# Pooled attention and a max-out feed-forward layer on one core: where key turns and one token turn stand in a hand-written order, and which engine copies the keys

## The chip, the cores and the metric

The kernel runs on one core of one Trainium2 chip. The metric is the device time of one execution in microseconds (us). The kernel before took 227.16 us, the median of three runs (226.39 to 227.36). All times inside an execution are counted from the start of the profiled span.

## The reference

The inputs are q, k and v of shape (8 batches, 8 heads, 576 tokens, 64), and four weights. Keys and values are averaged over groups of 8 tokens, which leaves 72 pooled keys and values per head; then comes ordinary attention, and a layer that takes the largest of three products.

```python
k_p = k.reshape(B, H, Sp, pool, D).mean(axis=3)
v_p = v.reshape(B, H, Sp, pool, D).mean(axis=3)
attn = softmax(q @ k_p.transpose(0, 1, 3, 2) / sqrt(D))
x = (attn @ v_p).transpose(0, 2, 1, 3).reshape(B * S, H * D)     # 4608 x 512
h = maximum(maximum(x @ w1, x @ w2), x @ w3)                     # 4608 x 768
out = h @ w_out                                                  # 4608 x 512
```

## The kernel before

**Two streams of work.** Attention goes by batch b (0 to 7, 576 tokens each). The feed-forward layer goes by blocks n of 512 tokens (0 to 8). The attention of a batch feeds the block or two behind it. The program is written out in issue order: every engine takes its instructions in the order of the program, and waits inside them are semaphores.

**The steps of a batch b.** GpSimd loads `q`, `k`, `v` with a cast to 2 bytes (L73 to L100) and sums keys and values over each group of 8 in the helper at L157 (tiles `half`, then `kp` and `vp`). The step `T` (L349) turns the queries on the way by a transposing DMA on SyncE's queue, `qT<-qb`. The step `k` (L207) is the key turn: three TensorE transposes of `kp` into a PSUM tile `pkt` (L202), then four copies of `pkt` into `kz` (L213), each 64 partitions by 288 elements. `s0`, `s3`, `s6` are the scores (`psc`, L226) with their exponentials on ScalarE (`et`, L231). `v0` to `v4` are five chunks of 128 tokens: eight matmuls into `pav` (L302), a reciprocal (L310) and a product (L312) on VectorE, which gives `xn`. `x0` to `x4` turn each chunk into the token ring `xT`: for batches up to 2 with four TensorE transposes into `pxt` (L293) and a ScalarE copy (L296), for later batches with a transposing DMA on SyncE's queue (L287).

**The steps of a block n.** `h` is one product of the hidden layer: four matmuls of 512 columns into a tile `pw` (L419); of each pair the first is taken out of PSUM by ScalarE (`t`, L425), the second by VectorE (`hT`, L427). A block from 2 on has twelve. The output stage is the digits 1, 2, 6, 7, 5, 3, 4: seven products of ten matmuls each (L765). Products 1, 6, 5 and 3 use the PSUM bank `oA` one after another and are copied out by ScalarE (L776); product 2 uses `oB`, and 7 and 4 use `oC`, which VectorE adds to the output (L779). `a` and `b` steps are VectorE differences that feed the products, `f` steps are sums of weights. A minus behind a name issues the TensorE part, a plus the copy out of PSUM; with neither sign, both come at once.

**The order.** `MIDDLE` (L949) holds a string for each of the blocks 1 to 5, and `middle(n)` (L982) reads it out. A name without a batch means batch n+1. `q7<`, `k7<`, `v7<` issue loads on GpSimd, which wait for the last hidden product issued so far and for the last turned queries. `!` says that the next sum on GpSimd waits for VectorE's last difference. After block 5 another string, `ORDER`, takes over.

**PSUM** has 8 banks. In this part of the program `att` is two tiles of two banks (scores, `pav`, `pxt` of batch 2, and `pkt`), `pw` three tiles of one bank (hidden products, `oB` and `oC`), `tr` one bank (`oA`). The tiles of a tag go round in order: a new one waits until the one two (`att`) or three (`pw`) places earlier has been read.

Of the kernel before, what the change touches and what calls it, by code (L numbers as in the profile page):

```python
# [14 lines left out]
def kernel(  # L15
# [11 lines left out]
    nc = tc.nc  # L27
# [3 lines left out]
    B, H, S, D = q.shape  # L31
# [167 lines left out]
    def keys(b, tag):  # L199
        pkt = psum([128, 3, 96], BF16, name="pkt", tag=tag[0], bufs=tag[1])  # L200
        for i in range(3):
            nc.tensor.transpose(pkt[:, i, :],  # L202
                                kps[b][:, 2 * i:2 * i + 2, :].rearrange("p i d -> p (i d)"),
                                ident[0:96, 0:96])
        return pkt

    def turn_k(b):  # L207
        pkt = keys(b, ATT if len(pools) < 3 else SC)

        def put():  # L210
            for par, evac in enumerate((nc.vector.tensor_copy, nc.scalar.copy)):
                for odd in range(2):
                    (evac if b > 2 else nc.vector.tensor_copy)(  # L213
                        out=kz_all[b % 2][par][64 * par:64 * par + 64, :, 0:Sp].rearrange(
                             "p h (r i t) -> p h r i t", i=3, t=2)[:, :, :, :, odd],
                        in_=pkt[64 * odd:64 * odd + 64].rearrange(
                             "p i (h r) -> p h r i", r=12))

        return put
# [100 lines left out]
    ATT = ("att", 2)  # L320
    ATT0, ONE = ("att", 3), ("one", 2)
    SC = ("sc", 2)
# [6 lines left out]
    def parts(name, begin):  # L329

        if name[-1] == "+":
            parked[name[:-1]].pop(0)()
        elif name[-1] == "-":
            parked.setdefault(name[:-1], []).append(begin())
        else:
            begin()()

    def do(b, steps):

        for name in steps.split():
            i = int(name[1:].rstrip("+-") or 0)
            if name[0] in "qQ":
                turn_q(b, *QS[i], nc.vector.tensor_copy if name[0] == "Q"
                       else nc.scalar.copy, TR)
            elif name[0] == "T":
                qTs[b] = sb2.tile([128, 2 * NG, 128], BF16, name="qT", tag="qT")
                turned[:] = [nc.sync.dma_start_transpose(  # L349
                    out=qTs[b], in_=qbs[b].rearrange("p hp t d -> p (hp t d)"))]  # L350
            elif name[0] == "k":
                parts(f"{b}:{name}", lambda: turn_k(b))
            elif name[0] == "K":
                fold_k(b, nc.vector)
            elif name[0] == "s":
                if i == 0 and name[-1] != "+":
                    new_et(b)
                if len(pools) == 3:
                    parts(f"{b}:{name}", lambda: scores_flat(b, i))
                elif name[-1] == "+":  # L360
                    parked[b, i].pop(0)()
                else:
                    ends = scores(b, {0: (0, 1, 2), 3: (4, 5, 3), 6: (6, 7)}[i])
                    if name[-1] == "-":
                        parked[b, i] = ends
                    else:
                        for end in ends:
                            end()
            elif name[0] == "d":
                for j in range(2):  # L370
                    sub_w(i, j, j + 1)
            elif name[0] == "S":
                next(out_sums, None)
            elif name[0] == "z":
                for par in range(2):
                    nc.vector.memset(kz_all[1][par], 0.0)
            elif name[0] == "w":
                turn_w(i, nc.scalar.copy if i % 2 else nc.vector.tensor_copy)
            elif name[0] == "v":
                parts(f"{b}:{name}", lambda: values(b, CHUNKS[i][0]))  # L380
            else:
                turn_x(b, *CHUNKS[i], xns[b, CHUNKS[i][0]], TR if b == 1 else ATT,
                       nc.vector.tensor_copy if name[0] == "X" else nc.scalar.copy)

    w1T = const.tile([128, JCH, C], F16, name="w1T", tag="w1T")
# [490 lines left out]

    folding = {}

    def pool_step(n, name):

        what, b = name[0], int(name[1])
        if name[2:] == "<":
            load = {"k": lambda: load_k(b, nc.gpsimd), "v": lambda: load_v(b, nc.gpsimd),
                    "q": lambda: load_q(b)}[what]
            op = load()
            for x in (mms[-1], *turned):
                after([op], x)
            return
        if (what, b) not in folding:
            if what == "k":  # L890
                new_kp(b)
                folding[what, b] = fold_steps(nc.gpsimd, kts[b], kps[b], parts=2)
            else:
                folding[what, b] = fold_steps(nc.gpsimd, vts[b], vp_all[:, b, :, 0:D],
                                                  parts=2)
        for _ in range(int(name[3:])):
            op = next(folding[what, b])
            for x in held:
                after([op], x)
            held.clear()  # L900
# [14 lines left out]
    def weave():  # L915

        products, seen, outs = {}, {}, out_seven(5)
        for name in ORDER.split():
            if name == "F":
                next(tiles)  # L920
            elif name == "vpool":
                held[:] = gate
                pool_step(5, "v7+4")
            elif name[0] == "b":
                sums_of(5, name)
            elif name == "H":
# [19 lines left out]
                else:  # L946
                    parts(name, begin)

    MIDDLE = {  # L949
        1: """  # L950
            h- q4< k4< h+ 1:x2 1:v4- h- h- v4< h+ 1:v4+ h+ h- 1:x3 h- h+ h+ h- 1:x4 h+ h- k-
            h- h+ h+ q0 h h- k+ h+ h q1 h s0- s0+ s0+ q2 h- s0+ h- s0+ h+ b1 S q3 h+ h- S S
            3:T S h+ a3 s3- a1 s3+ s3+ h- s3+ h- h+ h+ a2 h- s3+ a4 s6- s6+ 1- s6+ h+ b3 b2
            b4 v0 2- 1+ 6- x0 v1 7- v2- 6+ x1 5- 2+ 7+ v2+ ! k3+4 v3- v3+2 v3+ 5+ v4 3- x2
            4- x3 3+ 4+ x4
        """,
        2: """
            h k5< k- h- k+ h+ a1 a3 h- a2 f a4 f ! v3+2 v5< h+ f s0- s0+ s0+ s0+ h- h- h- h+
            h+ s0+ h- h+ s3- h+ h- f s3+ h- s3+ h+ h- s3+ b1 s3+ s6- h+ s6+ h- h+ h- s6+ !
            k4+2 h+ h+ b2 b3 b4 ! k4+2 1- 4:T v0- 1+ v1- v0+ x0 2- v1+ 6- v2- 7- x1 2+ 7+  # L960
            v4+2 6+ v2+ 5- v3- 5+ v3+ x2 x3 v4 x4 3- 4 3+
        """,
        3: """
            k- q5< k+ a3 k6< h a1 h- h- h+ a2 s0- f a4 ! v4+2 s0+ s0+ f h- h+ s0+ h+ s0+ h-
            h- h+ h+ s3- h- v6< h+ h s3+ s3+ s3+ s3+ h- b1 h- h+ h+ s6- s6+ ! k5+2 h h- s6+
            1- h+ b2 b3 b4 1+ ! k5+2 v5+2 v0- 2- v0+ x0 v1 6- 2+ x1 6+ 7- 5:T 7+ v2- 5- v2+
            x2 v3- 5+ v3+ v4 x3 3 x4 4
        """,
        4: """
            h- q6< h+ k- h- k+ a1 a2 f h+ h- a3 a4 ! v5+2 h- f h+ k7< h+ s0- s0+ h- h- s0+  # L970
            s0+ h+ s0+ h+ 6:T h- s3- h+ s3+ s3+ s3+ h- s3+ h+ h- b1 h+ h ! k6+2 s6- s6+ h h
            b3 b2 b4 s6+ ! k6+2 1- v6+2 v0 2- 1+ x0 v1- 6- v1+ 2+ x1 v2 7- 6+ 5- x2 v3 6:k-
            x3 7+ 5+ 3- 6:k+ v4 x4 4- 3+ 4+
        """,
        5: """
            h q7< a1 v7< h- a2 h- a3 h+ h+ a4 ! v6+2 h- s0- s0+ h+ s0+ h- s0+ s0+ h- h- k7+4
            h+ h+ s3- h+ 7:T s3+ h- s3+ h- s3+ s3+ h+ s6- h+ s6+ s6+ h h- v0 h+ h- x0 v1- h+
            v1+ x1
        """}
    folds = iter([f for wi in range(1, 3) for f in [fold_w(wi)] * 4])  # L980

    def middle(n):  # L982

        pieces, outs, out_tiles = hidden(n), None, project(n)
        for name in MIDDLE[n].split():
            if name[0] == "h":
                parts(name, lambda: next(pieces))
            elif name == "F":
                next(out_tiles)
            elif name == "f":  # L990
                next(next(folds))
            elif name == "!":
                held[:] = gate
            elif name[0].isdigit() and name[1:] in ("", "+", "-"):
                outs = outs or out_seven(n)
                parts(f"o{name}", lambda: outs(int(name[0]), 0, 1))
            elif name[0] in "ab":
                sums_of(n, name)
            elif name[2:3] == "<" or name[2:3] == "+" and name[3:]:
                pool_step(n, name)  # L1000
            else:
                b, _, step = name.rpartition(":")
                do(int(b or n + 1), step)
        assert next(pieces, None) is None

    tt_all.append(const.tile([128, 4, 5, HALF], F16, name="tt", tag="tt"))
    for n in range(1, 6):
        middle(n)
    assert next(folds, None) is None
    pad2 = const.tile([128, 3, 2, HALF], F16, name="pad2", tag="k16")  # L1010
    pad3 = ld.tile([128, 8, 2, HALF], F16, name="pad3", tag="vt")
# [47 lines left out]
```

## Time and profile before

| what | value |
|---|---|
| median of three runs | 227.16 us |
| the profiled execution's own time | 227.08 us |
| its span on the core | 225.4 us |
| TensorE matmul busy | 212.3 us (94%) |
| VectorE busy | 161.4 us (72%) |
| ScalarE busy | 120.3 us (53%) |
| GpSimd busy | 140.9 us (63%) |
| granted TensorE clock | 1.0 |
| key copies (L213) | 18 on VectorE of 478 ns, 10 on ScalarE of 476 ns |
| query turns by DMA (L349) | 5, from 4.0 to 10.2 us from issue to landing |

Three views are read below. The chain of waits follows the work that ended last back to the start, and tells at each step what released it. The timeline lists merged instructions: start, length, engine, line, operation, tiles, count, and in square brackets how long the engine was idle before and on whom it waited. The page's list of DMA issues gives the time from issue to landing. Matmul rows overlap, since each row includes the time until its result has landed: a group's start and the next group's start tell more than the length of the row.

### The profile page before, as it was taken

What the parts mean: (1) busy time and instruction counts of PE and PEld (TensorE: products, weight loads), DVE (VectorE), ACT (ScalarE), POOL (GpSimd) and SP (SyncE); (2) the same over time, 40 slices, a digit from 0 to 9 for tenths busy, and PEclk for the clock granted to TensorE, in tenths of its full rate; (3) what the DMA queues carried; (4) which work ended last, traced back from release to release, by engine and by line L of the source; (5) the groups of instructions that cost most, each with busy time, mean ns of one, the idle gap of its engine ahead of it and who ended that gap; (6) DMA issues with size and microseconds to landing.
All of it is one profiled execution on the core that took longest, in us unless ns stands there. A gap on an engine that the chain in (4) does not pass through costs nothing.

```text
span 225.4 us, 4876 instructions
## 1 busy us (share of the span) xinstructions
PE 212.3 (94%) x1884; PEld 147.1 (65%) x1885; DVE 161.4 (72%) x314; ACT 120.3 (53%) x233; POOL 140.9 (63%) x121
## 2 busy tenths in 40 slices
PE   6688999999999999999999999999799999999993
PEld 2477744458658645964685468547589667788882
DVE  3668898036997796776679668729767977878940
ACT  2267524855883576237724842693694445564330
POOL 7974300999939969775885769794292903881020
PEclk9999999999999999999999999999999999999999
DMA  6999999999649999649967999699530755200265
GB/s 179 209 197 197 211 203 209 202 168 230 115 105 156 168 176 247 122 61 214 252 85 154 221 202 151 86 236 166 109 56 19 163 102 113 47 0 3 66 198 159
DMA packets 47303, 33.55 MB, mean 149 GB/s; under 512 B 26992, under 2 KB 42288, under 8 KB 47280
## 3 DMA queue, kind: packets, MB, share of 16 engines
q0 software_dynamic: 16944, 16.98, 47.8%
q1 hardware_dynamic: 29888, 15.87, 31.1%
q10 hardware_dynamic: 448, 0.39, 0.7%
q8 instruction: 15, 0.25, 0.5%
q14 instruction: 8, 0.07, 0.1%
HBM read 34.60 MB, written 9.44 MB: 195 GB/s over the span
## 4 chain that ended last, share of the span: by engine, by line
PE 58%; DMA 17%; DVE 10%; POOL 7%; ACT 3%; issue 3%; ACTq 0%; POOLq 0%; DVEq 0%
PE pw L419 17%; PE oA L765 12%; DMA vt<-in_v_dram 8%; PE oC L765 6%; PE pA L842 5%; DMA mw<-in_moe_w_dram 4%; DMA qT<-qb 4%; PE oB L765 3%; PE pC L842 3%; PE pav L302 2%; PE po L471 2%; PE psc L226 2%; POOL half L163 2%; DVE kz L213 2%; DVE tt L664 1%
## 5 line engine op out<-in xcount | busy, mean ns | idle before, releaser
L419 PE MATMUL pw<-xT,mw 128*128 128x512 f16 (+1 forms) x336 | 68.5, 349 | 0.3 <-ACT xT L296 0.2
L419 PEld LDWEIGHTS <-mw 128*128 128x128 f16 x336 | 30.7, 98 | 26.1 <-issue 1.8
L163 POOL TENSOR_TENSOR half<-vt 72x1024 f32<-72x1024 f16 (+1 forms) x12 | 29.1, 2444 | 20.8 <-DMA vt<-in_v_dram 13.3
L427 DVE TENSOR_TENSOR hT<-t,pw 128x512 f16<-128x512 f16 (+1 forms) x42 | 25.3, 608 | 19.1 <-PE pw L419 11.3
L231 ACT ACTIVATE et<-psc 72x512 f16<-72x512 f32 (+2 forms) x66 | 33.9, 571 | 6.7 <-PE psc L226 6.5
L165 POOL TENSOR_TENSOR half<-half 72x1024 f32<-72x1024 f32 (+1 forms) x13 | 28.1, 2165 | 12.6 <-DVE tt L664 5.2
L425 ACT ACTIVATE t<-pw 128x512 f16<-128x512 f32 (+1 forms) x42 | 22.6, 538 | 15.1 <-PE pw L419 14.5
L312 DVE TENSOR_TENSOR xn<-pav,rcp 128x512 f16<-128x512 f32 x40 | 27.6, 691 | 1.4
L776 ACT COPY osb<-oA 128x512 f32<-128x512 f32 x20 | 11.7, 587 | 20.1 <-PE oA L765 19.9
L851 ACT CAST pad<-pA 128x512 f16<-128x512 f32 x27 | 15.1, 585 | 11.7 <-PE pA L842 9.1
L765 PEld LDWEIGHTS <-tt 128*128 128x128 f16 x200 | 18.8, 98 | 2.1
L163 POOL TENSOR_TENSOR half<-ktFalse 96x768 f32<-96x768 f16 (+1 forms) x11 | 19.3, 1773 | 0.6 <-issue 0.5
L226 PEld LDWEIGHTS <-kz 64*128 64x128 bf16 (+1 forms) x161 | 8.9, 95 | 12.4 <-issue 7.2
L302 PEld LDWEIGHTS <-et 72*128 72x128 f16 x320 | 14.9, 98 | 3.0 <-issue 1.1
L302 PE MATMUL pav<-vp,et 72*128 72x65 f16 x320 | 16.3, 194 | 0.6 <-POOL vp L167 0.3
L310 DVE RECIPROCAL rcp<-pav 128x8 f32<-128x8 f32 x40 | 8.1, 201 | 11.3 <-PE pav L302 11.2
L842 PEld LDWEIGHTS <-sw 128*128 128x128 f16 x144 | 13.8, 98 | 2.7 <-issue 0.2
L822 DVE SCALAR_TENSOR_TENSOR hT<-pad 128x512 f16<-128x512 f16 x18 | 14.0, 785 | 1.1 <-ACT pad L855 0.5
L819 DVE TENSOR_TENSOR pad<-pad,pC 128x512 f16<-128x512 f16 x18 | 12.3, 681 | 3.5 <-PE pC L842 2.7
L226 PE MATMUL psc<-qT,kz 64*128 64x256 bf16 (+5 forms) x138 | 13.3, 263 | 1.0 <-DVE qT L197 0.9
L616 POOL TENSOR_TENSOR pad<-xT 128x256 f16<-128x256 f16 x8 | 5.5, 687 | 13.1 <-DMA xT<-xn 13.1
L765 PEld LDWEIGHTS <-hT 128*128 128x128 f16 x126 | 12.3, 98 | 1.4
(122 smaller groups left out, 400.6 us busy)
## 6 DMA issues: line engine op xcount, KB each, us to landing
out_dram<-osb SPq DMA_DIRECT2D x32, 128.0 KB, 4.6
ktFalse<-in_k_dram POOLq DMA_DIRECT2D x7, 576.0 KB, 9.1
qb<-in_q_dram POOLq DMA_DIRECT2D x7, 576.0 KB, 7.6
vt<-in_v_dram POOLq DMA_DIRECT2D x7, 576.0 KB, 11.8
out_dram<-osb SPq DMA_DIRECT2D x11, 256.0 KB, 6.8
mw<-in_moe_w_dram POOLq DMA_DIRECT2D x9, 256.0 KB, 9.2
ktTrue<-in_k_dram SPq DMA_DIRECT2D x3, 384.0 KB, 5.1
out_dram<-ob SPq DMA_DIRECT2D x8, 128.0 KB, 2.9
```

Of the source, the lines that this page charges most:

```text
L163: yield e.tensor_tensor(out=f[:, at], in0=t[:, at, 0:4, :], in1=t[:, at, 4:8, :], op=ALU.add)
L165: yield e.tensor_tensor(out=f[:, :, 0:2, :], in0=f[:, :, 0:2, :], in1=f[:, :, 2:4, :], op=ALU.add)
L226: nc.tensor.matmul(out, kz_all[b % 2][f % 2][rows, h, :], qTs[b][rows, n + i0:n + i1, 64 * (h % 2):64 * (h % 2) + 64], start=True, stop=True)
L231: nc.scalar.activation(out=out, in_=in_, func=FT.Exp, scale=1.0 / 64.0)
L302: nc.tensor.matmul(pav[:, h // 4, 65 * (h % 4):65 * (h % 4) + 65], ets[b][:, h, c0:c0 + 128], vp_all[:, b, h, :], start=True, stop=True)
L312: nc.vector.tensor_tensor(out=xn, in0=pv[:, :, :, 0:D], in1=rcp.to_broadcast([128, 2, 4, D]), op=ALU.mult)
L419: mm = nc.tensor.matmul(pw, w_sb[wi][:, kc, bass.ts(jc, 128)], x[:, kc], start=(kc == 0), stop=(kc == KCH - 1))
L425: yield lambda t=t, pw=pw: nc.scalar.activation(out=t, in_=pw, func=FT.Relu)
L427: yield lambda t=t, pw=pw: nc.vector.tensor_tensor(out=hT[:, jc, c0:c1], in0=t, in1=pw, op=ALU.max)
L765: nc.tensor.matmul(p, left, right, stop=(r == 4), skip_group_check=True, start=(i in FIRST and r == 0 and (m == 0 or n == LAST)))
L842: mm = nc.tensor.matmul(p[:, w], a[:, kc, bass.ts(g, 128)], b[:, kc, :], start=(i in FIRST and w + kc == 0), stop=(w + kc == 2), skip_grou ...
L851: nc.scalar.copy(out=kept(i, g), in_=p)
```

## The change

Four things change; the loads, the sums, the products and all arithmetic stay as they are.

1. The key turns of batches 4, 5 and 6 take their PSUM tile from `pw` in place of `att`, and all four of their copies are on ScalarE, where two were on VectorE and two on ScalarE. Batches 3 and 7 keep two and two, earlier ones four on VectorE.
2. These three key turns stand elsewhere, and are no longer in two parts. Batch 4's moves from behind block 2's output stage to behind `v4` of batch 3, ahead of block 2's product 3. Batch 5's moves from behind the first hidden product of block 4 to behind `v4` of batch 4, ahead of block 3's product 3. Batch 6's moves by a little: it stays ahead of block 4's product 3, and `v4` of batch 5 now stands ahead of that product too.
3. The token turn `x2` of batch 2 moves from behind block 1's product 3 to ahead of it (and ahead of `v4`), and takes its PSUM tile from `pw`.
4. In batch 2, `v1` and `x0` change places.

The five strings become one with the block's number ahead of a slash; the steps are otherwise the same and in the same order. The core of the diff, with the strings cut to the stretches that differ (the old ones written with the same block and batch numbers):

```diff
+    KP = (4, 5, 6,)
+
     def turn_k(b):
-        pkt = keys(b, ATT if len(pools) < 3 else SC)
+        pkt = keys(b, PW if b in KP else SC if len(pools) == 3 else ATT)
...
-            for par, evac in enumerate((nc.vector.tensor_copy, nc.scalar.copy)):
+            for par in range(2):
                 for odd in range(2):
-                    (evac if b > 2 else nc.vector.tensor_copy)(
+                    (nc.vector.tensor_copy if b < 3 else nc.scalar.copy if par or b in KP
+                     else nc.vector.tensor_copy)(
...
-                turn_x(b, *CHUNKS[i], xns[b, CHUNKS[i][0]], TR if b == 1 else ATT,
+                turn_x(b, *CHUNKS[i], xns[b, CHUNKS[i][0]],
+                       TR if b == 1 else PW if (b, i) == (2, 2) else ATT,
...
-  1/6- 2:x0 2:v1 1/7- 2:v2-
+  1/6- 2:v1 2:x0 1/7- 2:v2-
...
-  1/5+ 2:v4 1/3- 2:x2 1/4- 2:x3 1/3+ 1/4+ 2:x4 2/h
+  1/5+ 2:x2 2:v4 1/3- 1/4- 2:x3 1/3+ 1/4+ 2:x4 2/h
...
-  2/5+ 3:v3+ 3:x2 3:x3 3:v4 3:x4 2/3- 2/4 2/3+ 4:k- q5< 4:k+ 3/a3 k6< 3/h
+  2/5+ 3:v3+ 3:x2 3:x3 3:v4 4:k 3:x4 2/3- 2/4 2/3+ q5< 3/a3 k6< 3/h
...
-  3/5+ 4:v3+ 4:v4 4:x3 3/3 4:x4 3/4 4/h- q6< 4/h+ 5:k- 4/h- 5:k+
+  3/5+ 4:v3+ 4:v4 5:k 4:x3 3/3 4:x4 3/4 4/h- q6< 4/h+ 4/h-
...
-  5:x2 5:v3 6:k- 5:x3 4/7+ 4/5+ 4/3- 6:k+ 5:v4 5:x4 4/4- 4/3+ 4/4+ 5/h
+  5:x2 5:v3 4/7+ 4/5+ 6:k 5:x3 5:v4 4/3- 5:x4 4/4- 4/3+ 4/4+ 5/h
```

More of the change, by code (lines that the diff above doesn't have):

```diff
@@ L877, with pool_step @@
     folding = {}
-    def pool_step(n, name):
+    def pool_step(name):
         what, b = name[0], int(name[1])
@@ L922, in weave @@
                 held[:] = gate
-                pool_step(5, "v7+4")
+                pool_step("v7+4")
             elif name[0] == "b":
@@ L947, in weave @@
                     parts(name, begin)
[L949 to L979, printed above, removed]
@@ L980 @@
-    folds = iter([f for wi in range(1, 3) for f in [fold_w(wi)] * 4])
[L982 to L990, printed above, removed]
+    MIDDLE = """
+        1/h- q4< k4< 1/h+ 1:x2 1:v4- 1/h- 1/h- v4< 1/h+ 1:v4+ 1/h+ 1/h- 1:x3 1/h- 1/h+ 1/h+
+        1/h- 1:x4 1/h+ 1/h- 2:k- 1/h- 1/h+ 1/h+ 2:q0 1/h 1/h- 2:k+ 1/h+ 1/h 2:q1 1/h 2:s0-
+        2:s0+ 2:s0+ 2:q2 1/h- 2:s0+ 1/h- 2:s0+ 1/h+ 1/b1 S 2:q3 1/h+ 1/h- S S 3:T S 1/h+ 1/a3
+        2:s3- 1/a1 2:s3+ 2:s3+ 1/h- 2:s3+ 1/h- 1/h+ 1/h+ 1/a2 1/h- 2:s3+ 1/a4 2:s6- 2:s6+ 1/1-
+        2:s6+ 1/h+ 1/b3 1/b2 1/b4 2:v0 1/2- 1/1+ 1/6- 2:v1 2:x0 1/7- 2:v2- 1/6+ 2:x1 1/5- 1/2+
+        1/7+ 2:v2+ ! k3+4 2:v3- v3+2 2:v3+ 1/5+ 2:x2 2:v4 1/3- 1/4- 2:x3 1/3+ 1/4+ 2:x4 2/h
+        k5< 3:k- 2/h- 3:k+ 2/h+ 2/a1 2/a3 2/h- 2/a2 f 2/a4 f ! v3+2 v5< 2/h+ f 3:s0- 3:s0+
+        3:s0+ 3:s0+ 2/h- 2/h- 2/h- 2/h+ 2/h+ 3:s0+ 2/h- 2/h+ 3:s3- 2/h+ 2/h- f 3:s3+ 2/h-
+        3:s3+ 2/h+ 2/h- 3:s3+ 2/b1 3:s3+ 3:s6- 2/h+ 3:s6+ 2/h- 2/h+ 2/h- 3:s6+ ! k4+2 2/h+
+        2/h+ 2/b2 2/b3 2/b4 ! k4+2 2/1- 4:T 3:v0- 2/1+ 3:v1- 3:v0+ 3:x0 2/2- 3:v1+ 2/6- 3:v2-
+        2/7- 3:x1 2/2+ 2/7+ v4+2 2/6+ 3:v2+ 2/5- 3:v3- 2/5+ 3:v3+ 3:x2 3:x3 3:v4 4:k 3:x4 2/3- 2/4 2/3+ q5< 3/a3 k6< 3/h 3/a1 3/h- 3/h- 3/h+ 3/a2 4:s0- f 3/a4 ! v4+2 4:s0+
+        4:s0+ f 3/h- 3/h+ 4:s0+ 3/h+ 4:s0+ 3/h- 3/h- 3/h+ 3/h+ 4:s3- 3/h- v6< 3/h+ 3/h 4:s3+
+        4:s3+ 4:s3+ 4:s3+ 3/h- 3/b1 3/h- 3/h+ 3/h+ 4:s6- 4:s6+ ! k5+2 3/h 3/h- 4:s6+ 3/1- 3/h+
+        3/b2 3/b3 3/b4 3/1+ ! k5+2 v5+2 4:v0- 3/2- 4:v0+ 4:x0 4:v1 3/6- 3/2+ 4:x1 3/6+ 3/7-
+        5:T 3/7+ 4:v2- 3/5- 4:v2+ 4:x2 4:v3- 3/5+ 4:v3+ 4:v4 5:k 4:x3 3/3 4:x4 3/4 4/h- q6< 4/h+ 4/h- 4/a1 4/a2 f 4/h+ 4/h- 4/a3 4/a4 ! v5+2 4/h- f 4/h+ k7< 4/h+ 5:s0- 5:s0+
+        4/h- 4/h- 5:s0+ 5:s0+ 4/h+ 5:s0+ 4/h+ 6:T 4/h- 5:s3- 4/h+ 5:s3+ 5:s3+ 5:s3+ 4/h- 5:s3+
+        4/h+ 4/h- 4/b1 4/h+ 4/h ! k6+2 5:s6- 5:s6+ 4/h 4/h 4/b3 4/b2 4/b4 5:s6+ ! k6+2 4/1-
+        v6+2 5:v0 4/2- 4/1+ 5:x0 5:v1- 4/6- 5:v1+ 4/2+ 5:x1 5:v2 4/7- 4/6+ 4/5- 5:x2 5:v3 4/7+ 4/5+ 6:k 5:x3 5:v4 4/3- 5:x4 4/4- 4/3+ 4/4+ 5/h q7< 5/a1 v7< 5/h- 5/a2 5/h- 5/a3
+        5/h+ 5/h+ 5/a4 ! v6+2 5/h- 6:s0- 6:s0+ 5/h+ 6:s0+ 5/h- 6:s0+ 6:s0+ 5/h- 5/h- k7+4 5/h+
+        5/h+ 6:s3- 5/h+ 7:T 6:s3+ 5/h- 6:s3+ 5/h- 6:s3+ 6:s3+ 5/h+ 6:s6- 5/h+ 6:s6+ 6:s6+ 5/h
+        5/h- 6:v0 5/h+ 5/h- 6:x0 6:v1- 5/h+ 6:v1+ 6:x1
@@ L991, in middle @@
+    """
+    folds = iter([f for wi in range(1, 3) for f in [fold_w(wi)] * 4])
+    def middle():
+        pieces, outs = {}, {}
+        for name in MIDDLE.split():
+            n, _, step = name.rpartition("/")
+            n = int(n or 0)
+            if step[0] == "h":
+                if n not in pieces:
+                    pieces[n] = hidden(n)
+                parts(name, lambda: next(pieces[n]))
+            elif step == "f":
                 next(next(folds))
-            elif name == "!":
+            elif step == "S":
+                next(out_sums)
+            elif step == "!":
@@ L993, in middle @@
                 held[:] = gate
[L994 to L1000, printed above, removed]
-            else:
-                b, _, step = name.rpartition(":")
-                do(int(b or n + 1), step)
@@ L1004, in middle @@
-        assert next(pieces, None) is None
+            elif n and step[0].isdigit():
+                if n not in outs:
+                    outs[n] = out_seven(n)
+                parts(name, lambda: outs[n](int(step[0]), 0, 1))
+            elif step[0] in "ab":
+                sums_of(n, step)
+            elif step[2:3] == "<" or step[2:3] == "+" and step[3:]:
+                pool_step(step)
+            else:
+                b, _, step = step.rpartition(":")
+                do(int(b), step)
@@ L1006 @@
+        assert all(next(p, None) is None for p in pieces.values())
     tt_all.append(const.tile([128, 4, 5, HALF], F16, name="tt", tag="tt"))
-    for n in range(1, 6):
-        middle(n)
+    middle()
     assert next(folds, None) is None
```

## The prediction

> **What bounds the kernel now.** I read the page first: TensorE is busy for 94% of the span at a granted clock of 1.0. So I asked next for what TensorE waited on, from 56 us (the end of block 0) to 160 us, which covers all that the change touches. Columns: total us, times, longest.
>
> ```profile
> PE psf L226 <- DMA qT<-qb: 1.6, 1, 1.6
> PE oA L765 <- ACT osb L776: 0.7, 4, 0.3
> ```
>
> There are two kinds: one long wait for turned queries, and four equal short ones in the output stage. The chain of waits (start, length, what) says which of them sets the end:
>
> ```profile
> 148.84 1.67 PE pw L419 x8
> 150.51 9.21 DMA qT<-qb
> 159.85 0.38 PE psf L226 x2
> ```
>
> The chain is almost only TensorE from 80 to 150 us, then leaves it for 9.21 us. TensorE goes on working meanwhile, arrives about 1.6 us too early and stands. So time saved on TensorE before 158 us counts only as far as this transfer comes earlier too. The timeline shows what starts it:
>
> ```profile
> 138.28 0.42 PE L302 MATMUL pav<-vp,et 72*128 72x65 f16 x8
> 138.54 0.29 PE L202 MATMUL pkt<-ident,kp 96*128 96x96 bf16 x3
> 139.11 0.60 PE L765 MATMUL oA<-so,xT 128*128 128x256 f16 x4 [0.28 <-ACT osb L776]
> 141.56 3.62 PE L419 MATMUL pw<-xT,mw 128*128 128x512 f16 x16
> 142.89 0.79 POOL L99 DMA_DIRECT2D qb<-in_q_dram  x1 [0.96 <-PE pw L419]
> 150.51 7.15 SPq L349 DMA_TRANSPOSE qT<-qb  x1
> 159.85 0.38 PE L226 MATMUL psf<-qT,kz 128*128 128x320 bf16 x2 [1.60 <-DMA qT<-qb]
> ```
>
> Batch 7's query load is issued at 142.89, when the first hidden product of block 5 (begun 141.56) is done; it lands 7.6 us later, which lets the turn go at 150.51, and that lands 9.2 us later. GpSimd had been free for 0.96 us. **The end therefore follows the moment at which block 5's first hidden product ends**, and I sum what the change does to that moment.
>
> **The sum, stage by stage.** Rows of matmuls overlap, so a group's cost is start to next start: a hidden product 0.86 us, an output product 1.09, a key turn 0.13 (98.26 to 98.39), eight `pav` 0.26, one `pxt` turn 0.23.
>
> *Block 1's output stage, gain 0.44.* Two holes. The product at 68.26 ends its work at 69.35, but `x0` starts at 69.56, held by `xn` (VectorE until 69.51). With `v1` first, its 0.26 fills the 0.21. `x0` then starts at 69.61, `xn` being ready. What follows moves by 0.21, which puts the start of product 5 at 71.43. Sixteen `pav` from 72.73 are through at 73.25; product 3 starts at 73.56, when ScalarE has emptied `oA`. In the new order product 5 is followed by `v3`, `x2`, `v4` (0.26 + 0.23 + 0.26), through at 73.27; ScalarE's copy, 1.29 after the start of product 5 as before, ends at 73.30 and product 3 starts at 73.35: 0.21 earlier. `x2`'s 0.23 no longer follows it: 0.44. For `x2`, `xn` of `v2` must be ready; I place it at 72.3 from VectorE's rows, `x2` at 72.78. Its `pw` tile was read long before. But the tile pushes the ring on by one: the second hidden product of block 2, and no longer the third, takes the tile of `oC`. VectorE's addition empties that at 76.40 at the latest; the product would start at 76.97. No cost.
>
> *Block 2's output stage into block 3, gain 0.24.* Here the rows are:
>
> ```profile
> 95.24 0.68 PE L302 MATMUL pav<-vp,et 72*128 72x65 f16 x16
> 95.44 0.58 ACT L776 COPY osb<-oA 128x512 f32<-128x512 f32 x1 [1.86 <-PE oA L765]
> 96.08 0.60 PE L765 MATMUL oA<-so,xT 128*128 128x256 f16 x4 [0.15 <-ACT osb L776]
> 98.26 0.29 PE L202 MATMUL pkt<-ident,kp 96*128 96x96 bf16 x3
> 98.46 0.69 DVE L779 TENSOR_TENSOR osb<-osb,oC 128x512 f32<-128x512 f32 x1
> 99.06 0.96 DVE L213 COPY kz<-pkt 64x288 bf16<-64x288 bf16 x2
> 100.12 0.96 ACT L213 COPY kz<-pkt 64x288 bf16<-64x288 bf16 x2 [2.17 <-DVE kz L213]
> 101.10 0.60 ACT L425 ACTIVATE t<-pw 128x512 f16<-128x512 f32 x1
> 101.75 1.46 PE L419 MATMUL pw<-xT,mw 128*128 128x512 f16 x6
> ```
>
> `pav` is through at 95.76, so 0.32 is empty before 96.08. The key turn's 0.13 goes into it, and the first hidden product of block 3 starts at 98.26 in place of 98.39. The second now needs `oC`'s tile: VectorE's addition ends at 99.15, so it starts at 99.20 and not at 99.12; 0.05 is left of the 0.13. Then a second gain: in the rows above, ScalarE's two key copies stand until 101.08 ahead of `t`, which frees the tile for the hidden product at 101.75. Scores started at 101.07; elsewhere a hidden product follows 0.49 after such a start (104.44 to 104.92), here 0.68. That 0.19 goes, since the four ScalarE copies (4 x 0.48 = 1.92) now run from 96.05 to 98.0. 0.05 + 0.19 = 0.24; without the wait for `oC` it would be 0.32.
>
> *Block 3's into block 4, gain 0.05.* Again 0.32 is empty (117.36 to 117.68), and 0.13 of key turn leaves 120.72. But `oC` is emptied at 120.06 + 0.69 = 120.75, so the second hidden product starts at 120.80 in place of 120.85. Without that wait it would be 0.13.
>
> *Block 4's, gain 0.27 at the load.* The key turn stays ahead of product 3, `v4`'s eight `pav` join it: 138.67 + 0.26 = 138.93 is still inside the hole that ends at 139.11. Old, `v4` stood behind, at 140.20. So the first hidden product of block 5 starts at 141.29 and not 141.56. This one needs no `oC`.
>
> Sum: 0.44 + 0.24 + 0.05 + 0.27 = **1.00 us**. The profiled execution took 227.08 us (span 225.4, 1.7 around it): 227.08 - 1.00 = 226.08, so **226.1**. The median shown, 227.16, is 0.08 above it; I don't correct for that.
>
> **What I cost at nothing.** *ScalarE's added copies*: 0.96 per turn, behind the copy of product 5 and ahead of that of product 3. That last one ends near 98.6, 120.2, 141.6; the next user of `oA` comes at 110, 132, 154, and the next `t` is due at 99.3, 120.9, 142.3. The tightest cover is 0.7 us; if it went, each turn would hold a hidden product for the excess. A key copy is 478 ns on VectorE and 476 on ScalarE, so nothing is lost by the engine. *VectorE* loses 0.96 per turn, but waits for TensorE at those places. *The moved wait*: a key turn ahead of product 3 waits for `kp`. GpSimd finishes it at 94.66, 116.11 and 137.65; the turns would come at 95.76, 117.36 and 138.54, so 0.9 to 1.2 us is spare. Behind a late one stand product 3 and all of TensorE. *GpSimd* is gated by VectorE's differences with 1.5 to 3.5 us idle in each block, so it comes along. *SyncE's queue*: no transfer is moved past another; only the stores of block 4 may start some 0.6 earlier, beside the load.
>
> **What the transfer can do.** No row shows this load and turn 1 us earlier. The bounds: from load issue to turned queries, 16.8 us for batch 7, and 17.6 for batch 6 (122.28 to 139.9). The turn alone took 4.0 to 10.2. I take 16.8, the nearest row.
>
> The DMA busy share is 0.87 from 141.9 to 150.5 and 1.21 (rows overlap) until 157.7: the transfers may be what fills this time. Then an earlier issue within the same traffic wins nothing; only what moves all the traffic counts, which is 0.73 of the sum and not block 4's 0.27. The Trainium skill says so of the chip: "DMA: Bandwidth & Descriptors", section "Issuing engines are not separate DMA queues", holds that transfers from any engine run on the same 16 DMA engines and interleave. By that rule the sum is 0.73, by the row of batch 7 alone 1.00.
>
> **Rivals.** (1) *Traffic-bound turn*: 227.08 - 0.73 = 226.35. For it: the share of 1.21. Against: 0.87 during the load. (2) *More*: `oC`'s tile holds nothing, which gives back 0.05 + 0.08, and the turn lands sooner. TensorE alone would allow 1.6 more. The point where it starts is 1.13 us, or 225.95; with a turn 0.5 sooner 225.5. (3) *Nothing arrives*: the load and turn take 17.6 as batch 6's did, 227.08 - 1.00 + 0.80 = 226.9. (4) *Slower: late keys*. If GpSimd's `kp` comes over 1.2 us later against TensorE, each of three turns stops TensorE ahead of product 3; 2 us late costs 0.8 to 1.1 each, some 2.8 in all, less 1.00: 228.9. Against it stand the idle times of GpSimd. (5) *It doesn't do what it says*: the hole before product 3 stays, since the `oA` copy sets it; only what stood behind moves. That is in the sum.
>
> **Chances.** Forecast 0.45, (1) 0.15, (2) 0.20, (3) 0.12, (4) 0.08. 0.5% is 1.14 us, about what a measurement of this kernel can tell from no change. The forecast is so near to it that a sixth of its chance lies beyond: faster 0.20 + 0.08 = 0.28; slower 0.08; within, 0.64. The three runs of before spread by 0.97 us. The range reaches from rival (2)'s 225.4 to 227.3, past (3) by half that spread.
>
> **What would show it.** The `oA` waits of blocks 1 and 4 shrink below 0.2; the `ACT kz <- DVE kz` wait goes for batches 4 to 6; the query load of batch 7 is issued near 141.9 and the first `psf` starts near 158.9. I am wrong if `pkt` rows wait for GpSimd, if the second hidden product of a block waits for `osb` L779 by more than 0.1, or if load and turn take other than 16.8 us.

## The result, and the profile after

The changed kernel takes 226.19 us (median of 22 runs), the kernel before 227.12 (22 runs): ratio 0.9958, 95% interval 0.9941 to 0.9975, a gain of 0.93 us. The prediction was 226.1. The profiled execution took 226.36 us, its span is 224.5.

The same two views of the changed kernel as ahead of the prediction. First what TensorE waited for from 56 to 160 us (total us, times, longest):

```profile
PE psf L229 <- ACT osb L780: 1.5, 1, 1.5
PE psc L229 <- ACT kz L215: 0.2, 1, 0.2
```

The four waits of `oA` are gone from the list. The second line, 0.2 us ahead of batch 3's scores, is a wait for key copies that the change leaves alone; in the kernel with the batch 2 part alone (below) the shift is 0.33 ahead of it and 0.31 behind it. The long one before `psf` is still there, under another name: ScalarE's copy of `osb` happens to end at 158.96, just behind the landing of the query turn at 158.93. The chain of waits follows the same name (start, length, what):

```profile
157.38 0.47 ACT kz L215
157.87 0.47 ACT kz L215
158.37 0.59 ACT osb L780
159.07 0.38 PE psf L229 x2
```

Of several semaphores that an instruction waits for, the view names the one that came last, and 0.03 us decide here. But in both kernels `psf` starts 0.14 us behind that landing, and the `osb` copy is not an input of `psf`. I read it as the same wait for the same transfer; the experiments bear that out.

The timeline at the end of block 4:

```profile
138.01 0.29 PE L202 MATMUL pkt<-ident,kp 96*128 96x96 bf16 x3
...
138.14 0.42 PE L305 MATMUL pav<-vp,et 72*128 72x65 f16 x8
...
138.43 1.95 ACT L215 COPY kz<-pkt 64x288 bf16<-64x288 bf16 x4
...
138.59 0.60 PE L769 MATMUL oA<-so,xT 128*128 128x256 f16 x4
...
139.06 0.68 DVE L783 TENSOR_TENSOR osb<-osb,oC 128x512 f32<-128x512 f32 x1
...
139.79 0.60 PE L769 MATMUL oC<-wm,tt 128*128 128x256 f16 x4
...
140.88 3.62 PE L423 MATMUL pw<-xT,mw 128*128 128x512 f16 x16
...
142.22 0.79 POOL L99 DMA_DIRECT2D qb<-in_q_dram  x1 [0.80 <-PE pw L423]
...
143.44 0.85 POOL L91 DMA_DIRECT2D vt<-in_v_dram  x1 [0.44 <-issue]
...
149.44 7.44 SPq L352 DMA_TRANSPOSE qT<-qb  x1
```

`v4`'s `pav` now stands between the key turn and product 3, and all four key copies are on ScalarE. But product 3 takes 1.09 us and product 4 (139.79) comes 1.20 behind it: it waits for VectorE's addition at 139.06, which empties `oC` of product 7. The rows of the start of block 3:

```profile
95.68 0.29 PE L202 MATMUL pkt<-ident,kp 96*128 96x96 bf16 x3
...
95.99 0.60 PE L769 MATMUL oA<-so,xT 128*128 128x256 f16 x4
...
96.01 1.95 ACT L215 COPY kz<-pkt 64x288 bf16<-64x288 bf16 x4
...
98.17 2.75 PE L423 MATMUL pw<-xT,mw 128*128 128x512 f16 x12
...
98.38 0.69 DVE L783 TENSOR_TENSOR osb<-osb,oC 128x512 f32<-128x512 f32 x1
...
99.24 0.60 ACT L429 ACTIVATE t<-pw 128x512 f16<-128x512 f32 x1 [0.67 <-PE pw L423]
...
101.34 1.90 PE L423 MATMUL pw<-xT,mw 128*128 128x512 f16 x8
```

`t` comes at 99.24 in place of 101.10, and the hidden product behind the scores at 101.34 in place of 101.75.

**A scale for what follows.** The two executions differ by 0.23 us before anything has changed (64.28 and 64.51 at the start of the last hidden product of block 1). So all places below are counted from there, in each kernel, and compared on the same footing. Shift of the changed kernel against the one before:

| place | predicted | measured |
|---|---|---|
| block 2, first hidden product | -0.44 | -0.33 |
| block 3, fourth hidden product | -0.68 | -0.64 |
| block 4, second hidden product | -0.73 | -0.75 |
| block 5, first hidden product; batch 7's query load | -1.00 | -0.91 |
| landing of batch 7's query turn | -1.00 | -1.01 |
| first `psf` | -1.00 | -1.01 |
| start of the last matmul | -1.00 | -1.02 |

### The profile page after: what moved, and what is told of

It reads as the page before. It is cut to its first block, busy times and chain, and to the rows that moved or that the text cites. A ratio compares the mean times of both kernels' runs of the same rounds, so it can differ in the third digit from the quotient of the medians.

```text
span 224.5 us, 4870 instructions
## 1 busy us (share of the span) xinstructions
PE 213.0 (95%) x1884; PEld 147.3 (66%) x1885; DVE 157.9 (70%) x308; ACT 123.2 (55%) x239; POOL 140.9 (63%) x121
## 4 chain that ended last, share of the span: by engine, by line
PE 69%; DMA 12%; POOL 8%; DVE 6%; ACT 2%; issue 1%; POOLq 0%; DVEq 0%; ACTq 0%
PE pw L423 22%; PE oA L769 13%; DMA vt<-in_v_dram 8%; PE oC L769 7%; PE pA L846 6%; DMA mw<-in_moe_w_dram 4%; PE pav L305 4%; PE oB L769 3%; PE psc L229 3%; PE po L475 3%; PE pC L846 3%; POOL half L163 2%; PE po L471 2%; DVE xn L315 1%; POOL mw L108 1%
```

## The experiments

Each kernel was run beside the kernel before; times are medians with the ratio to it. Single effects of 0.1 to 0.6 us are below what these times tell apart, so the experiments are read at the places of the scale, in one profiled execution of each kernel.

### The two halves of the change

The diffs against the changed kernel undo the keys, and batch 2:

```diff
-    KP = (4, 5, 6,)
+    KP = ()
...
-  3:v4 4:k 3:x4 2/3- 2/4 2/3+ q5< 3/a3
+  3:v4 3:x4 2/3- 2/4 2/3+ 4:k- q5< 4:k+ 3/a3
```

```diff
-  1/6- 2:v1 2:x0 1/7- ... 1/5+ 2:x2 2:v4 1/3- 1/4-
+  1/6- 2:x0 2:v1 1/7- ... 1/5+ 2:v4 1/3- 2:x2 1/4-
-                       TR if b == 1 else PW if (b, i) == (2, 2) else ATT,
+                       TR if b == 1 else ATT,
```

(Batches 5 and 6 go back likewise in the first.)

> Only the batch 2 part of the change (v1 ahead of x0, x2 ahead of product 3 of block 1 with its tile from pw); key turns of batches 4 to 6 as before. Read at places on TensorE, against the kernel before, with the difference at the end of block 0 taken off. Theory (holes filled, and the shift carried to the end by batch 7's query load): block 2's first hidden product 0.34 us earlier, the same 0.3 at block 5's first hidden product, at the load and at the end, 226.8. Rival (all gain comes from the key copies): block 2 earlier, but nothing left at block 5 and at the end, 227.1.

> Only the key part (places, pw tile, ScalarE copies of batches 4 to 6); batch 2 as before. Theory: nothing at block 2's first hidden product, 0.31 by block 3's fourth hidden product, 0.44 at block 4's second, 0.59 at block 5's first and at the load, 0.6 to 0.7 at the end, 226.5. Rival (the parts depend on each other): the sum of this and of the batch 2 part differs from the whole by more than 0.1 at block 5's first hidden product.

| kernel | us | ratio (interval) | block 2 | block 3 | block 4 | block 5 | `psf` |
|---|---|---|---|---|---|---|---|
| batch 2 alone | 227.03 | 0.9986 (0.9958 to 1.0015) | -0.33 | -0.31 | -0.31 | -0.30 | -0.65 |
| keys alone | 226.87 | 0.9992 (0.9963 to 1.0022) | 0.01 | -0.30 | -0.42 | -0.57 | -0.77 |
| both (the change) | 226.19 | 0.9958 (0.9941 to 0.9975) | -0.33 | -0.64 | -0.75 | -0.91 | -1.01 |

The parts add up, as expected: 0.30 + 0.57 = 0.87 against 0.91 at block 5. A rival in which only the keys count, or the parts lean on each other, falls. At `psf` they don't add up (0.65 + 0.77 against 1.01): the landing of the transfer differs by some tenths from kernel to kernel.

### Which engine copies, and which tile is taken

```diff
-                    (nc.vector.tensor_copy if b < 3 else nc.scalar.copy if par or b in KP
+                    (nc.vector.tensor_copy if b < 3 else nc.scalar.copy if par
```

> The changed kernel, with the key copies of batches 4 to 6 split again, two on VectorE and then two on ScalarE; place and pw tile as changed. Against the changed kernel, with the difference at the end of block 0 taken off. Theory (ScalarE's pair must wait for VectorE's, which stands behind the product of v4; the copy of product 3 and the next t stand behind both): fourth hidden product 0.2 later in block 3 and 0.7 later in block 4, nothing in block 5; 0.9 at block 5's first hidden product and at the load. Rival (only place and tile matter): under 0.1 everywhere.

Measured: 228.38 us, ratio 1.0050 (1.0023 to 1.0076), slower than the kernel before. In the profiled execution block 5 comes 1.93 later than in the changed kernel, twice what I expected: 0.97 at the second hidden product of block 3 and 0.96 at that of block 4. The kernel's timeline:

```profile
98.22 1.03 PE L423 MATMUL pw<-xT,mw 128*128 128x512 f16 x4
...
98.31 0.97 DVE L215 COPY kz<-pkt 64x288 bf16<-64x288 bf16 x2
...
99.30 0.69 DVE L783 TENSOR_TENSOR osb<-osb,oC 128x512 f32<-128x512 f32 x1
...
99.36 0.96 ACT L215 COPY kz<-pkt 64x288 bf16<-64x288 bf16 x2 [3.37 <-DVE kz L215]
...
100.05 1.89 PE L423 MATMUL pw<-xT,mw 128*128 128x512 f16 x8 [0.80 <-DVE osb L783]
```

VectorE's pair puts the emptying of `oC` back to 99.99, and the second hidden product stands until then: here it does take `oC`'s tile. In the changed kernel it does not: the semaphores that it waits for there are ScalarE's and TensorE's own, and VectorE's stand at the third, as in the kernel before. Strictly in turn, the second product would get `pkt`'s tile in both kernels, since `pkt` stands between the `oC` of product 7 and that of product 4. In both, the tile that is handed on is the one whose last reader ends first: `pkt` at 97.96 ahead of `oC` at 99.07 in the changed kernel, `oC` at 99.99 ahead of `pkt` at 100.32 here. So tiles do not always go round in turn, as the paragraph on PSUM has it; how the program comes to this order is not shown.

The second edit puts the tile back, with the places and ScalarE's copies kept:

```diff
-        pkt = keys(b, PW if b in KP else SC if len(pools) == 3 else ATT)
+        pkt = keys(b, ATT if b in KP else SC if len(pools) == 3 else ATT)
```

> The changed kernel, with the key turns of batches 4 to 6 in att tiles again; place and ScalarE copies as changed. Against the changed kernel, with the difference at the end of block 0 taken off. Theory (the tile is what makes the place possible): batch 4's turn waits for VectorE's product of v3, product 3 of block 2 comes 1.7 later; in block 3 1.5 later; in block 4 v4 waits, 0.9 later; near 4 us at block 5, end 229 to 230. Rival (att has a tile free there): under 0.3 in all.

Measured: 231.32 us, ratio 1.0165 (1.0127 to 1.0204). What TensorE waited for between 93 and 150 us:

```profile
PE pkt L202 <- DVE rcp L313: 3.6, 2, 1.8
PE pav L305 <- DVE xn L315: 0.9, 1, 0.9
```

The waits are the expected ones. In the profiled execution block 5 came 7.7 later all the same, not 4: behind each of the two long stops the granted TensorE clock was halved for 3.41 us (below). That execution took 233.82 us, the longest of six. In the two shortest, 230.08 and 230.54 us, the mean granted clock was 1.0; they lie 3.9 and 4.4 above the changed kernel's median, close to the 4 expected.

### What the end follows

The prediction's last link was "load issue, plus 16.8 us". Four kernels pull at it. First the query load alone, then the values load behind it:

```diff
-  4/4+ 5/h q7< 5/a1 v7<
+  4/4+ q7< 5/h 5/a1 v7<
```

> The changed kernel, with batch 7's query load issued ahead of block 5's first hidden product in place of behind it, so that it no longer waits for that product. Against the changed kernel. Theory (the end follows the moment of this load): GpSimd's 0.80 idle before the load goes, load, turn and first psf come 0.8 earlier, end 0.8 earlier, 225.4; TensorE still stands about 0.85 before psf. Rival (the transfers fill the time, traffic sets the turn's landing): load 0.8 earlier, but the turn lands within 0.3 of where it did, end within 0.3.

```diff
-  ! k6+2 4/1- v6+2 ... 5/h q7< 5/a1 v7<
+  ! k6+2 4/1- q7< v6+2 ... 5/h 5/a1 v7<
```

> The changed kernel, with batch 7's query load issued ahead of the sum of batch 6's values on GpSimd. Against the changed kernel. Theory: the load waits only for batch 6's turn, which lands at 138.2, so it is some 4 us earlier; the turn then waits for SyncE's stores (until 145.7) and lands near 155; TensorE no longer stands before psf, which comes 1.5 us earlier, and so does the end: 224.7. Rival (traffic): the turn lands at most 0.5 earlier, end 225.7 or later.

```diff
-  5/h q7< 5/a1 v7< 5/h- ... k7+4 5/h+
+  5/h q7< 5/a1 5/h- ... k7+4 v7< 5/h+
```

> The changed kernel, with batch 7's values load moved from right behind batch 7's query load to behind the sum of batch 7's keys on GpSimd (about 154.3). In five kernels so far batch 7's query turn landed 1.9 to 2.0 us after that values load, whenever the turn was issued. Theory now (the values load is what the turn lands behind): the turn lands by 156, TensorE no longer stands before psf, which comes about 1.5 us earlier than in the changed kernel; end up to 1.5 earlier, 224.7, unless the later values stop the sum of batch 7's values at 161. Theory of the prediction (load issue plus 16.8): the turn lands within 0.4 of 158.9, end unchanged.

And the 0.12 that the new wait for `oC` costs, as a small pull at block 5's first hidden product:

```diff
-  5:x2 5:v3 4/7+ 4/5+ 6:k 5:x3 5:v4
+  5:x2 5:v3- 4/7+ 4/5+ 6:k 5:v3+ 5:x3 5:v4
```

> The changed kernel, with batch 5's v3 copy-out moved behind the copy-out of block 4's product 5, so that VectorE adds oC before it takes v3. Against the changed kernel, with the difference at the end of block 0 taken off. Theory (block 4's product 4 now waits 0.12 for VectorE's addition of product 7, which stands behind the product of v3): product 4 no longer waits, block 5's first hidden product 0.1 earlier; end within 0.2. Rival (the 0.12 has another cause): no difference at block 5's first hidden product, or later.

Shifts against the changed kernel; the last two columns are the length of the turn from issue to landing, and how long behind the landing of the values load it landed:

| kernel | us, ratio (interval) | query load | turn lands | `psf` | last matmul | turn | behind values |
|---|---|---|---|---|---|---|---|
| before | 227.12 | 0.91 | 1.01 | 1.01 | 1.02 | 9.21 | 2.00 |
| changed | 226.19, 0.9958 (0.9941 to 0.9975) | 0 | 0 | 0 | 0 | 9.49 | 1.95 |
| load as free | 225.88, 0.9946 (0.9920 to 0.9972) | -0.85 | -0.74 | -0.67 | -0.73 | 9.78 | 1.98 |
| load early | 227.37, 1.0014 (0.9980 to 1.0049) | -3.43 | -1.11 | 0.16 | 0.06 | 11.67 | 1.94 |
| `oC` first | 226.30, 0.9956 (0.9935 to 0.9976) | -0.12 | 0.11 | 0.11 | 0.20 | 10.03 | 1.86 |
| values load late | 228.00, 1.0042 (1.0016 to 1.0068) | 0.30 | -3.25 | -0.38 | 1.67 | 5.99 | lands first |

The row *load as free* looks like the prediction's theory. But its values load is issued 0.48 earlier too. *Load early* speaks plainly: the turn is issued 3.3 earlier and lands 1.1 earlier, because it takes 11.67 us; it still lands 1.94 behind the values. (`psf` does not follow even that: GpSimd finishes batch 7's `kp` 1.65 later in this kernel, and `psf` waits 0.7 for the key copies.) `oC` first gains its 0.11 at block 5 and at the load, as expected, and loses it at the landing. *Values load late* decides: issued at nearly the same moment, the turn takes 5.99 us. (The 0.30 in the first column of this row is older than the edit: `v2` of batch 3 waited 0.29 for VectorE, where the two programs are still the same.) SyncE's queue, in the changed kernel and in that one:

```profile
149.44 7.44 SPq L352 DMA_TRANSPOSE qT<-qb  x1
156.98 1.21 SPq L290 DMA_TRANSPOSE xT<-xn  x1
```

```profile
149.31 3.92 SPq L352 DMA_TRANSPOSE qT<-qb  x1
153.47 1.19 SPq L290 DMA_TRANSPOSE xT<-xn  x1
```

So **the turn lands behind the values load that was issued ahead of it**, 1.8 to 2.0 us behind in all ten kernels with this order. (Batch 4's turn is issued 3.9 us ahead of a values load, and lands ahead of it: at 92.15 and 94.04 in the changed kernel.) The load of the queries only had to be early enough. The rows show where the time goes. SyncE's issue of the turn takes 7.44 us in one kernel and 3.92 in the other, and the landing comes 2.1 us behind the end of the issue in both. In all fourteen kernels the issue of batch 7's turn ends within 0.3 us of the landing of the last transfer issued ahead of it. In the changed kernel this is the values load, which lands at 156.98; in the other it is a store, which lands at 153.20. Batch 6's turn does the same in all of them, in the changed kernel behind a load of keys (134.69, the landing at 134.62). So in *load early* the earlier turn takes longer to issue, 9.63 us. Why the issue is held so long is not shown.

"DMA: Bandwidth & Descriptors" of the Trainium skill, section "Queues, rings and completion order", gives a mechanism for transfers that share the engines: each DMA engine goes round its queues packet by packet, and drains a whole packet before it turns to the next. No run here changes the packet size, so that this is the reason for the delay is argued and not shown.

Why did the end not follow in *values load late*? `psf` came only 0.38 earlier although the turn landed 3.25 earlier, since batch 7's key copies are next (`PE psf` waited 0.82 there on `ACT kz`; in *load as free* it already starts 0.05 behind these copies and 0.21 behind the turn); and then GpSimd's sum of those values starts late:

```profile
162.60 4.19 POOL L163 TENSOR_TENSOR half<-vt 72x1024 f32<-72x1024 f16 x2 [7.83 <-DMA vt<-in_v_dram]
```

TensorE stops 2 us for `v0` of batch 7. The load in two halves, batch 7's key copies on ScalarE right behind their turn, and both with `oC` first, were meant to take these away in turn:

```diff
-  "v": lambda: load_v(b, nc.gpsimd),
+  "v": lambda: load_v(b, nc.gpsimd, cuts=(0, 4, 8) if b == 7 else (0, H)),
```

```diff
-                    (nc.vector.tensor_copy if b < 3 else nc.scalar.copy if par or b in KP
+                    (nc.vector.tensor_copy if b < 3 else nc.scalar.copy if par or b > 3
...
-  o1+ k7- b2 1a- 1b- v62- 1a+ k7+ 2a+
+  o1+ k7 b2 1a- 1b- v62- 1a+ 2a+
```

> As the kernel with the late values load of batch 7, but that load in two halves of four heads, so that GpSimd can begin the sum with the first half. Against the changed kernel, with the difference at the end of block 0 taken off. Theory: the turn lands near 155.5 as there, psf comes 0.7 earlier (it then waits for batch 7's key copies), and this 0.7 reaches the end, since the sum starts in time: 225.5. Rival (the late values load costs by its whole length, not by the start of the sum): the stop of 2 us before v0 of batch 7 stays, end 1.3 later as there.

> As the kernel with the late values load in two halves, and in addition batch 7's key copies all on ScalarE, right behind the key turn. Against the changed kernel, with the difference at the end of block 0 taken off. Theory (next late behind the turn are these copies, VectorE's pair and then ScalarE's): psf 1.5 earlier, when TensorE arrives; of that 1.2 to 1.5 at the end, 224.8, since the second half of the values may hold the sum by some tenths. Rival (ScalarE's added copies hold block 6's products): psf earlier, but what follows loses it again; end within 0.3 of the kernel with the halves alone.

> The changed kernel with batch 7's key copies all on ScalarE right behind the key turn, and the values load where the changed kernel has it. Against the changed kernel, with the difference at the end of block 0 taken off. Theory (the query turn lands behind the values load, near 159, and sets psf): psf and the end within 0.2. Rival (the key copies set psf in the changed kernel): psf and the end 0.5 or more earlier.

> As the kernel with the late values load in two halves and batch 7's key copies on ScalarE, and in addition the copy-out of v3 of batch 5 behind that of block 4's product 5. Theory: the 0.12 gained at block 5's first hidden product now reaches the end, 0.1 earlier than without it. Rival: nothing, or a loss of up to 0.3 behind it.

| kernel | us, ratio (interval) | turn lands | `psf` | last matmul |
|---|---|---|---|---|
| values late, in halves | 226.54, 0.9964 (0.9944 to 0.9984) | -3.55 | -0.67 | 0.31 |
| the same, last keys on ScalarE | 226.36, 0.9971 (0.9947 to 0.9995) | -4.04 | -1.66 | 0.06 |
| last keys on ScalarE alone | 226.34, 0.9963 (0.9941 to 0.9985) | -0.23 | -0.23 | -0.21 |
| all three | 226.43, 0.9961 (0.9939 to 0.9983) | -4.43 | -1.40 | 0.40 |

*Last keys alone* is the control: with the turn where it was, `psf` starts 0.13 behind its landing, and the key copies count for nothing. With the turn out of the way they are worth 1 us at `psf` (-0.67 to -1.66), which is what TensorE can use. It is lost at once. What TensorE waited for from 150 to 200 us in that kernel:

```profile
PE oB L769 <- DVE pad L823: 0.9, 1, 0.9
PE psf L229 <- ACT et L234: 0.5, 1, 0.5
PE pC L846 <- DVE pad L823: 0.4, 1, 0.4
PE pav L305 <- POOL vp L167: 0.4, 1, 0.4
```

The four key copies hold ScalarE's copy out of block 6's first product, VectorE's addition behind that comes late, and `oB` waits 0.9; then 0.4 for the values. The halves alone did not help as meant: they landed within 0.3 us of each other (162.0 and 162.3). On the common scale the sum began 0.76 earlier than in *values load late* (its older 0.29 taken off), and TensorE's stop for `v0` shrank from 2.0 us to 0.9 without going. In the last kernel the expectation for `oC` failed too: block 5's first hidden product came 0.26 later, having waited for a token turn by DMA, which it did not in the kernel with that edit alone. None of these beats the changed kernel. *Load as free* has the best median; its interval and the changed kernel's overlap almost wholly, so that it is better is not shown.

## Why the prediction came out right, and where its steps did not

**The total was right, 1.00 against 0.93 by the medians**, and so, up to the last link, was the way to it: holes ahead of products whose bank ScalarE empties, filled with work that stood behind, and a shift that reaches the end because batch 7's loads shift with it. Term by term:

- *Block 1: 0.44 predicted, 0.33 measured.* Both holes were filled: product 3 came 0.22 earlier, 0.21 predicted. Then product 4 had to wait 0.115 for VectorE's addition of `oC`, which `x2` had covered. I had looked at what is late next ahead of product 3, and not behind it.
- *Block 4: 0.27 predicted, 0.15 measured at block 5's first hidden product*, for the same reason, 0.12 on `oC`. `oC` first shows it: with VectorE's addition ahead of `v3`, block 5's first hidden product comes 0.11 earlier.
- *Block 2 into 3: 0.24 predicted, 0.31 measured; block 3 into 4: 0.05 predicted, 0.12 measured.* The step that failed is "The second now needs `oC`'s tile". `pkt`'s is handed on first, and `oC`'s goes to the third, as before. Counted in turn, as the prediction assumed, it would have been the same; the count was one place off. The prediction had named both values without that wait (0.32 and 0.13), and they were the right ones. (Its rival (2) gives back 0.05 + 0.08 for this; by its own rows it is 0.08 + 0.08.) The two kinds of error cancel, -0.23 and +0.14, and that is luck.
- *ScalarE's copies at nothing:* right, and more than that. With two of the four on VectorE the change becomes a loss (1.0050), which the prediction did not say: it saw VectorE relieved of work that nobody waited for, but behind the new places stands the emptying of `oC`.
- *The wait for `kp`:* right. No `pkt` row of the changed kernel waits for GpSimd; rival (4) didn't come up.
- *"The end therefore follows the moment at which block 5's first hidden product ends":* right in the sum, wrong as a mechanism. The load and turn took 16.7 us against 16.8, but not because each has its own length. The turn lands behind the values load, and this is issued 1.2 us behind the query load in both kernels, so the two readings give the same number for this change. To that extent the number held by luck. Rival (1) had the mechanism, the shared transfers, and drew the wrong sum from it: it kept block 4's gain from the end, although the values load gets that gain too. The landing moved by 1.01 and block 5 by 0.91; the 0.10 between them is a values load and a turn a little shorter in this execution, which the sum does not hold.

## What to carry to other kernels

A hole that an in-order engine leaves behind a full bank can be filled with a step that stands behind it, if that step has an operand ready, a tile of its own, and a copying engine that isn't due for the next bank; the wait behind the next product must be looked at as well. Where a chain of waits leaves the compute engines for a transfer, ask which other transfers were issued ahead of it and are still under way: the end may follow the last of those, and an earlier issue then buys little. In an experiment of some tenths of a microsecond, count from a place ahead of the edit: executions of these two kernels differed by 0.23 us before the first difference.

## What was not expected of the hardware

A stop of TensorE of just under 2 us can cost more than itself. In the profiled execution of the kernel with `att` tiles, two stops of 1.81 us (idle time, as the views give it) were each followed by 3.41 us in which the granted clock was halved; in the one with the copies split, a stop of 1.88 us before `psf` was. Its timeline shows it, ten output matmuls of 256 columns in 2.13 us (161.81 to 163.94) and not 1.09:

```profile
161.43 0.59 PE L229 MATMUL psf<-qT,kz 128*128 128x320 bf16 x2 [1.88 <-DMA qT<-qb]
161.81 1.06 PE L769 MATMUL oB<-wm,xT 128*128 128x256 f16 x4
162.66 1.48 PE L769 MATMUL oB<-mwo,hT 128*128 128x256 f16 x6
163.94 1.06 PE L846 MATMUL pA<-pad,sw 128*128 128x256 f16 x4
```

That is 1.6 of the 3.9 us by which the last matmul is late in this execution (230.28 us, the longest of twelve; their median is 228.38). Behind block 0, no stop of 1.72 us or less had that effect in any of the profiles, and one of 2.00 us had not either. Nor does the same stop have it each time: the six executions of the kernel with `att` tiles had mean granted clocks of 1.0 (two), 0.992 to 0.993 (three) and 0.985 (the profiled one). Half the clock for 3.41 of some 230 us lowers the mean by 0.007, so I estimate no halving, one and two. What decides is not shown. The Trainium skill, "TensorE: Matmul & The Clock Gate", section "HAM oscillation — how this bites in real kernels", sets the limit at idle gaps over some 3.4 us. Here gaps of 1.81 us were enough in one execution; the measurement decides. The stop before `psf`, 1.60 us in the kernel before and 1.49 in the changed one, is not far from there.
